# Mean squares of tokens summed straight onto all partitions in an attention and two-layer MLP kernel

## The chip, the core and the metric

The kernel runs on one core of one Trainium2 chip. The metric is the device time of one execution in microseconds (us); the median of three timed runs of the kernel before is 725.94 us (723.27 to 726.9). TensorE is written PE in the profile (PEld are its weight loads), VectorE is DVE, ScalarE is ACT, GpSimd is POOL, and SP issues the DMAs.

## The reference, cut to what matters

Landmark attention over 4 batches, 8 heads and 576 tokens gives one row of 512 numbers for each of 2304 tokens. Each row is divided by its root mean square, then goes through a gated layer, and last through a layer of eight experts for some of the tokens:

```python
x = attn_out.transpose(0, 2, 1, 3).reshape(B * S, H * D)      # 2304 x 512
rms = np.sqrt(np.mean(x * x, axis=-1, keepdims=True) + 1e-06)
xn = x / rms * rms_g
g = xn @ w_gate
silu = g * (1.0 / (1.0 + np.exp(-g)))
x = (silu * (xn @ w_val)) @ w_out                              # then the experts
```

The change is inside the first two lines, for one batch of 576 tokens at a time.

## The kernel before

**Stages.** Attention is never written out as 512 numbers per token. For each batch, `attention(b)` (line 556) leaves a matrix `AT` of 128 partitions by 2 by 576 tokens (heads and landmarks on the partitions) and a small matrix `WT`. The product of `WT` with the weights of the gated layer (`products`, tiles `P`) makes that layer's weights for this batch, so that its matmuls take `AT`, scaled per token, as their moving operand. The scale per token is `rbs`, 128 partitions by 576 tokens: the inverse root mean square of each token, the same on all partitions. `prep(half)` (line 709) multiplies `AT` by `rbs` into `ap` and splits `ap` into a high and a low part (`ap_t`) for one half batch.

The 2304 tokens pass as eight units of 288 (half a batch each). `run_unit` (line 1196) runs the two gated matmuls per chunk of 128 features (`pg`, `pv`, into `h`, split into `h_t`), twelve chunks, then the output projection (`o`, from `h_t` and `wo`, into `x2T`). The attention of the next batch, the products `P` and the routing run as side work between the matmuls of a unit. After the eighth unit a loop over pairs of expert and batch (`ph`, `py`) fills the last 160 us or so.

**The place of the change.** For each batch the last part of `attention` gets squares `sq` whose sum over partitions is 512 times the mean square of a token: two tiles of 128 by 576 in the first batch (`fast`), one in the others. Lines 673 to 680 sum them with the squares as the stationary operand and one column of `onesd` (each 1/512) as the moving one: five groups of tokens, each giving one column of `ps` with tokens on partitions. Lines 681 to 688 take `max` with 0 (not in the first batch), root and reciprocal on 128 by 4 and 64 by 1 numbers. Lines 691 to 703 bring the inverses back onto all partitions: a matmul per group of 128 tokens with the column of `rms` broadcast over 128 columns as the stationary operand and the identity as the moving one, then two copies, of 256 tokens by DVE and 320 by ACT, into `rbs`.

**What sets the order.** The code records instructions with their dependences, and a list scheduler of the framework orders each engine's queue by its own estimates of their lengths. Each engine then runs its queue strictly in that order. The helper `Paced` (line 36) calls every operation from line 58, so nearly all rows of the profile carry L58, and names of tiles tell the places apart. `Paced` also counts estimated lengths, by which `slot` (line 1178) decides how much side work is recorded between the matmuls of a unit. A matmul of two fp32 operands shows as two MATMUL records.

**What the steps touch besides.** `convert_w` and `convert_wout` (lines 768 and 778) turn the 64-bit weights into fp32 with VectorE and ScalarE: TENSOR_SCALAR, SCALAR_TENSOR_TENSOR and TENSOR_TENSOR on `wo`, `wf` and `x` are theirs on VectorE. They fill the stretch up to about 156 us, that is, unit 0. `rsplit` (line 80) casts a tile on ScalarE and subtracts on VectorE or GpSimd. A product `P` takes two PSUM banks of the pool `pb`, which has two, so the next product waits until VectorE has subtracted (`P<-P,P`) both.

Of the kernel before, what the change touches and what calls it, by code (L numbers as in the profile page):

```python
# [6 lines left out]
F32 = mybir.dt.float32  # L7
F32R = mybir.dt.float32r
I32 = mybir.dt.int32
ALU = mybir.AluOpType  # L10
AF = mybir.ActivationFunctionType
# [10 lines left out]
NH = S // 2  # L22
# [40 lines left out]
def attention_moe_kernel(  # L63
# [4 lines left out]
    V, A, G, PE = (  # L68
        Paced(e, busy, n)
        for e, n in (  # L70
            (nc.vector, "V"), (nc.scalar, "A"), (nc.gpsimd, "G"), (nc.tensor, "P")
        )
    )
# [3 lines left out]
    def pool(stack, name, bufs=1, **kw):  # L77
        return stack.enter_context(tc.tile_pool(name=name, bufs=bufs, **kw))
# [37 lines left out]
    sm = pool(pha, "sm", side="right")  # L116

    start, start1 = ExitStack(), ExitStack()
# [6 lines left out]
    def atile(name):  # L125
        if fast:
            return st0.tile([128, S], F32, name=name, tag="wa", bufs=6)
        return at.tile([128, S], F32, name=name, tag="wa", bufs=2)

    def atbank(name):  # L130
        nonlocal nbank
        nbank += 1
        if fast and nbank % 4 < 2:
            return accbank(name)
        if fast and nbank % 4 == 2:
            return bank(name)
        return pa.tile([128, 512], F32, name=name, tag="a")

    def accbank(name):
        return acc.tile([128, 512], F32, name=name, tag="acc")  # L140

    def bank(name):
        return pb.tile([128, 512], F32, name=name, tag="b")
# [5 lines left out]
    ident = const.tile([128, 128], F32, name="ident")  # L149
# [8 lines left out]
    onesd = const.tile([128, 32], F32, name="onesd")  # L158
# [10 lines left out]
    eps = const.tile([128, 1], F32, name="eps")  # L169
# [48 lines left out]
    rbs = big.tile([128, S], F32, name="rbs")  # L218
# [337 lines left out]
    def attention(b, convs=()):  # L556
# [31 lines left out]
        if fast:  # L588
# [25 lines left out]
            for g in range(2):  # L614
                for p in range(2):
                    sq = atile("sq")
                    for t in range(2):
                        ps = atbank("oT")
# [3 lines left out]
                            start=True, stop=True,  # L622
                        )
                        A.activation(sq[:, NH * t : NH * t + NH], ps[:, 0:NH], AF.Square)
                    i = 2 * g + p
                    if i < 2:
                        sqs.append(sq)
                    else:
                        o = sqs[i % 2]
                        V.tensor_tensor(o, o, sq, ALU.add)  # L630
                    yield
        else:
# [29 lines left out]
            for g in range(2):  # L662
                sq = atile("sq")
                for t in range(2):
                    ts = slice(NH * t, NH * t + NH)
                    ps = atbank("sq")
# [3 lines left out]
                yield  # L670
            V.tensor_tensor(sqs[0], sqs[0], sqs.pop(), ALU.add)

        ps = atbank("ms")
        tiles = [(t, 128 if t < 4 else 64) for t in range(5)]
        for t, m in tiles:
            for i, sq in enumerate(sqs):
                PE.matmul(
                    ps[0:m, t : t + 1], sq[:, 128 * t : 128 * t + m], onesd[:, 0:1],
                    start=(i == 0), stop=(i == len(sqs) - 1),
                )  # L680
        rms = sm.tile([128, 5], F32, name="rms")
        for sl in ((slice(0, 128), slice(0, 4)), (slice(0, 64), slice(4, 5))):
            ms = ps[sl]
            if not fast:
                ms = rms[sl]
                V.tensor_scalar(ms, ps[sl], 0.0, None, ALU.max)
            A.activation(rms[sl], ms, AF.Sqrt, bias=eps[sl[0]])
            V.reciprocal(rms[sl], rms[sl])
        yield

        for i, ts in enumerate((tiles[0:2], tiles[2:5])):
            ps = atbank("rb")
            n = sum(m for t, m in ts)
            for t, m in ts:
                o = 128 * (t - 2 * i)
                PE.matmul(
                    ps[:, o : o + m], rms[0:m, t : t + 1].to_broadcast([m, 128]),
                    ident[0:m, 0:m], start=True, stop=True,
                )
            if i:  # L700
                A.copy(rbs[:, 256 : 256 + n], ps[:, 0:n])
            else:
                V.tensor_copy(rbs[:, 0:n], ps[:, 0:n])
        yield


# [513 lines left out]
    def first_convs():  # L1220
        for i in range(NC0):
            convert_w(i)
            yield

    drain(attention(0, first_convs()))
    G.memset(wcat, 0.0)
    SP.dma_start(wcat[:, :, 0:E], w_gate2.rearrange("(c p) e -> p c e", p=128))
# [22 lines left out]
    fast = False  # L1250
    prep(1)
    att = attention(1)
    raw = None

# [41 lines left out]
    for u in range(1, 2 * B):  # L1296
# [24 lines left out]
        if half == 0 and b + 1 < B:  # L1321
            att = attention(b + 1)
# [69 lines left out]
```

## Time and profile before

| | us |
|---|---|
| median of the timed runs | 725.94 |
| lowest and highest | 723.27, 726.9 |
| the profiled execution | 730.47 |
| its span | 728.7 |
| PE busy | 667.1 (92%) |
| DVE busy | 459.2 (63%) |
| ACT busy | 295.1 (41%) |

The profiled execution is 0.6% above the median; 1.8 us of its time lie outside the span. Busy shares are over the whole span, and the stages differ: up to about 85 us PE has little to do, up to 156 us (unit 0) the conversions of weights fill DVE, and later PE is busy nearly all the time.

### The profile page before, as it was taken

Reading aid. Unit: us, or ns where it says so; the run is one execution under the profiler, and the core shown is the slowest. Engines: PE = TensorE matmul, PEld = TensorE weight load, DVE = VectorE, ACT = ScalarE, POOL = GpSimd, SP = SyncE. Lnnn points to the kernel's source line nnn. Section 1 sums busy time; section 2 is a strip of 40 time slices with the busy share of each in tenths; the row PEclk is TensorE's granted clock in tenths of the full one; section 3 lists DMA queues with packets and bytes.
Section 4 is the critical chain, followed back from the end, with each engine's and each line's share of the span. In section 5 each row is a group of like instructions: output and inputs, shape, how many; then the busy total and the mean of one; then the engine's idle time right before and its main releaser. Section 6 shows DMA issues by size and latency. Waiting matters only on the chain. (4 is left out here: it accounts for less than half of the span.)

```text
span 728.7 us, 13382 instructions
## 1 busy us (share of the span) xinstructions
PE 667.1 (92%) x4961; PEld 573.5 (79%) x4961; DVE 459.2 (63%) x1016; ACT 295.1 (41%) x641; POOL 145.1 (20%) x162
## 2 busy tenths in 40 slices
PE   5468799789999899999999999999999999997997
PEld 5257367678877599977898897899889988986985
DVE  5984888978887577886467966261553463352451
ACT  0773887753314431433341344240443243241340
POOL 4000024313200140220040130040362023021120
PEclk8765799899999999999999999999999999998999
DMA  8686464573125842226732107230541375462344
GB/s 284 216 248 227 143 217 152 176 180 100 46 86 117 196 128 75 93 67 149 187 84 66 64 20 157 69 75 1 166 139 62 101 218 173 130 201 95 128 140 156
DMA packets 79435, 97.12 MB, mean 133 GB/s; under 512 B 16016, under 2 KB 58000, under 8 KB 79376
## 3 DMA queue, kind: packets, MB, share of 16 engines
q1 hardware_dynamic: 79376, 96.33, 44.9%
q8 instruction: 37, 0.61, 0.4%
q14 instruction: 22, 0.18, 0.1%
HBM read 76.97 MB, written 19.34 MB: 132 GB/s over the span
## 5 line engine op out<-in xcount | busy, mean ns | idle before, releaser
L58 PE MATMUL o<-h_t,wo 128*128 128x288 f32 x1152 | 169.6, 303 | 9.2 <-ACT wo L58 3.8
L58 PEld LDWEIGHTS o<-h_t,wo 128*128 128x128 f32 x1152 | 157.9, 191 | 19.2 <-issue 6.7
L58 POOL TENSOR_TENSOR h_t<-h,h_t 128x288 fp32r<-128x288 f32 x96 | 82.2, 860 | 399.9 <-ACT h_t L58 363.8
L58 PE MATMUL pg<-ap_t,P 128*128 128x288 f32 x576 | 104.1, 306 | 3.6 <-DVE h L58 1.8
L58 PE MATMUL pv<-ap_t,P 128*128 128x288 f32 x576 | 98.8, 301 | 2.7 <-DVE h L58 2.4
L58 PEld LDWEIGHTS pg<-ap_t,P 128*128 128x128 f32 x576 | 83.2, 189 | 17.6 <-issue 10.3
L58 PEld LDWEIGHTS pv<-ap_t,P 128*128 128x128 f32 x576 | 82.8, 189 | 8.8 <-DVE h L58 4.1
L58 PE MATMUL ph<-xsh,P 128*128 128x288 f32 x384 | 80.5, 303 | 4.5 <-PEq L1354 4.5
L58 PEld LDWEIGHTS ph<-xsh,P 128*128 128x128 f32 x384 | 64.0, 194 | 5.4 <-issue 5.4
L58 DVE SCALAR_TENSOR_TENSOR h<-h,pg 128x288 f32<-128x288 f32 x96 | 42.5, 447 | 26.3 <-ACT h L58 25.2
L58 PE MATMUL ph<-xsl,P 128*128 128x288 f32 x192 | 57.9, 302 | 0.0
L58 ACT ACTIVATE h<-pg 128x288 f32<-128x288 f32 x96 | 38.9, 410 | 42.4 <-PE pg L58 39.1
L58 ACT CAST h_t<-h 128x288 fp32r<-128x288 f32 x96 | 40.8, 430 | 32.6 <-DVE h L58 32.0
L58 PE MATMUL py<-wo,h_t 128*128 128x512 f32 x210 | 51.6, 395 | 0.3 <-DVE h_t L58 0.3
L58 PEld LDWEIGHTS py<-wo,h_t 128*128 128x128 f32 x210 | 39.3, 188 | 10.2 <-issue 0.8
L58 DVE TENSOR_TENSOR h<-h,pv 128x288 f32<-128x288 f32 x96 | 42.4, 446 | 5.9 <-PE pv L58 3.0
L58 DVE STREAM_TRANSPOSE T<-kq 64x576 f32<-64x576 f32 (+1 forms) x40 | 35.6, 889 | 9.0 <-DMA kq<-in_q_dram 4.6
L58 DVE TENSOR_TENSOR P<-P,P 128x512 fp32r<-128x512 f32 x48 | 31.7, 685 | 12.5 <-ACT P L58 12.1
L58 ACT CAST P<-P 128x512 fp32r<-128x512 f32 x48 | 26.3, 588 | 31.8 <-PE P L58 31.6
L58 PEld LDWEIGHTS ph<-xsl,P 128*128 128x128 f32 x192 | 37.4, 195 | 0.1
L58 POOL TENSOR_TENSOR P<-w1r,P 128x512 fp32r<-128x512 f32 x16 | 21.4, 1341 | 66.3 <-ACT P L58 66.3
L58 DVE SCALAR_TENSOR_TENSOR old<-py,mc,old 128x512 f32<-128x512 f32 (+1 forms) x18 | 13.5, 749 | 31.4 <-PE py L58 31.2
(230 smaller groups left out, 967.2 us busy)
## 6 DMA issues: line engine op xcount, KB each, us to landing
wl<-wg_d SPq DMA_DIRECT2D x36, 256.0 KB, 4.7
wr<-wv_d SPq DMA_DIRECT2D x32, 256.0 KB, 4.8
w1r<-in_moe_w_dram SPq DMA_DIRECT2D x32, 256.0 KB, 3.2
wr<-in_moe_w_gate_dram SPq DMA_DIRECT2D x6, 1024.0 KB, 6.6
wr<-in_moe_w_val_dram SPq DMA_DIRECT2D x6, 1024.0 KB, 6.1
wo<-in_moe_w_dram SPq DMA_DIRECT2D x24, 256.0 KB, 5.3
kq<-in_k_dram SPq DMA_DIRECT2D x8, 576.0 KB, 4.3
kq<-in_q_dram SPq DMA_DIRECT2D x8, 576.0 KB, 4.0
```

What stands on the lines that cost most here:

```text
L58: return f(*args, **kw)
```

## The change

The sum is done with the operands the other way round: the column of `onesd`, broadcast over 128 columns, is the stationary operand and the squares are the moving one. Each output partition then holds the mean square of every token, so the result is at once on all partitions, in two halves of 288 tokens. Root and reciprocal are taken on 128 by 288 numbers, into `rbs`. The matmuls with the identity, the two copies and the tile `rms` are gone.

```diff
-        ps = atbank("ms")
-        tiles = [(t, 128 if t < 4 else 64) for t in range(5)]
-        for t, m in tiles:
+        for t in range(2):
+            ts = slice(NH * t, NH * t + NH)
+            ps = atbank("ms")[:, 0:NH]
             for i, sq in enumerate(sqs):
                 PE.matmul(
-                    ps[0:m, t : t + 1], sq[:, 128 * t : 128 * t + m], onesd[:, 0:1],
+                    ps, onesd[:, 0:1].to_broadcast([128, 128]), sq[:, ts],
                     start=(i == 0), stop=(i == len(sqs) - 1),
                 )
-        rms = sm.tile([128, 5], F32, name="rms")
-        for sl in ((slice(0, 128), slice(0, 4)), (slice(0, 64), slice(4, 5))):
-            ms = ps[sl]
+            ms = ps
             if not fast:
-                ms = rms[sl]
-                V.tensor_scalar(ms, ps[sl], 0.0, None, ALU.max)
-            A.activation(rms[sl], ms, AF.Sqrt, bias=eps[sl[0]])
-            V.reciprocal(rms[sl], rms[sl])
-        yield
-
-        for i, ts in enumerate((tiles[0:2], tiles[2:5])):
-            ps = atbank("rb")
-            n = sum(m for t, m in ts)
-            for t, m in ts:
-                o = 128 * (t - 2 * i)
-                PE.matmul(
-                    ps[:, o : o + m], rms[0:m, t : t + 1].to_broadcast([m, 128]),
-                    ident[0:m, 0:m], start=True, stop=True,
-                )
-            if i:
-                A.copy(rbs[:, 256 : 256 + n], ps[:, 0:n])
-            else:
-                V.tensor_copy(rbs[:, 0:n], ps[:, 0:n])
+                ms = rbs[:, ts]
+                V.tensor_scalar(ms, ps, 0.0, None, ALU.max)
+            A.activation(rbs[:, ts], ms, AF.Sqrt, bias=eps)
+            V.reciprocal(rbs[:, ts], rbs[:, ts])
         yield
```

The scheduler makes a new order of everything near these places. Three of them follow.

On VectorE, first batch, before unit 0 (`wo<-wr` and `wo<-wo,s` are conversions of weights). Before:

```order
L58 TENSOR_SCALAR wo<-wr 128x1024
L58 RECIPROCAL rms<-rms 128x4
L58 RECIPROCAL rms<-rms 64x1
L58 SCALAR_TENSOR_TENSOR wo<-wr,wo 128x1024
L58 COPY rbs<-rb 128x256
L58 TENSOR_TENSOR ap<-AT,rbs 128x288 x4
L58 TENSOR_TENSOR ap_t<-ap,ap_t 128x288 x4
L58 TENSOR_TENSOR wo<-wo,s_873 128x1024
L58 TENSOR_TENSOR P_690<-P,P_690 128x512 x2
```

Now:

```order
L58 TENSOR_SCALAR wo<-wr 128x1024
L58 SCALAR_TENSOR_TENSOR wo<-wr,wo 128x1024
L58 RECIPROCAL rbs<-rbs 128x288 x2
L58 TENSOR_TENSOR wo<-wo,s_858 128x1024
L58 TENSOR_TENSOR ap<-AT,rbs 128x288 x3
L58 TENSOR_TENSOR ap_t<-ap,ap_t 128x288 x3
L58 TENSOR_TENSOR ap<-AT,rbs 128x288
L58 TENSOR_TENSOR P_675<-P,P_675 128x512 x2
```

The reciprocals stand behind one conversion, a second conversion stands between them and `ap`, and the copy is gone.

On VectorE at the end of unit 0, where `x2T<-o` is the first work on the output of the unit, `ln` and `lmk` are the landmarks of the next batch's second group of heads, and `mx`, `nmx` and `csum` its softmax. Before:

```order
L58 TENSOR_REDUCE ln<-kq 128x64
L58 TENSOR_TENSOR wo<-x_1234,wo 128x512
L58 STREAM_TRANSPOSE lmk_1511<-ln 128x64
L58 TENSOR_SCALAR x2T<-o 128x288 x2
L58 TENSOR_REDUCE mx<-sq 128x1 x2
L58 TENSOR_SCALAR nmx<-mx 128x1
L58 TENSOR_SCALAR csum<-cs 128x1
```

Now:

```order
L58 TENSOR_TENSOR wo<-x_1219,wo 128x512
L58 STREAM_TRANSPOSE lmq_1398<-ln 128x64
L58 TENSOR_TENSOR bdq<-lmq_1398,maskj 128x256
L58 TENSOR_SCALAR x2T<-o 128x288 x2
L58 TENSOR_REDUCE mx<-sq 128x1 x2
L58 TENSOR_SCALAR nmx<-mx 128x1
L58 TENSOR_REDUCE ln<-kq 128x64
L58 TENSOR_SCALAR csum<-cs 128x1
L58 STREAM_TRANSPOSE lmk_1496<-ln 128x64
```

A reduction over the keys has moved from before the last conversion of unit 0 to behind `nmx`, into unit 1.

On VectorE in the last batch, where `P<-P,P` are the subtractions that free the banks of the products. Before:

```order
L58 TENSOR_SCALAR rms<-ms 128x4
L58 TENSOR_SCALAR rms<-ms 64x1
L58 TENSOR_TENSOR P_690<-P,P_690 128x512 x2
L58 RECIPROCAL rms<-rms 128x4
L58 RECIPROCAL rms<-rms 64x1
L58 COPY rbs<-rb 128x256
L58 SCALAR_TENSOR_TENSOR h<-h,pg 128x288
L58 TENSOR_TENSOR ap<-AT,rbs 128x288 x2
L58 TENSOR_TENSOR P_690<-P,P_690 128x512
```

Now:

```order
L58 TENSOR_SCALAR rbs<-ms 128x288 x2
L58 TENSOR_TENSOR P_675<-P,P_675 128x512
L58 SCALAR_TENSOR_TENSOR h<-h,pg 128x288
L58 TENSOR_TENSOR h<-h,pv 128x288
L58 RECIPROCAL rbs<-rbs 128x288 x2
L58 TENSOR_TENSOR P_675<-P,P_675 128x512
L58 TENSOR_TENSOR ap<-AT,rbs 128x288 x2
L58 TENSOR_TENSOR P_675<-P,P_675 128x512
```

Both reciprocals stand directly ahead of the subtraction that frees the first bank of a product, and `ap` stands ahead of the one that frees the second.

On TensorE the `ms` rows become four matmuls of 128x288 in the first batch and two in each of the others, and the five `rb` matmuls are gone everywhere. Behind the fourth batch's place, around 460 us, the orders of all engines are the same as before but for two neighbours on VectorE that change places.

## Rows read from the trace of the kernel before

**Rows 1.** The page: busy time per engine, then three strips of 40 slices.

```profile
PE 667.1 (92%) x4961; PEld 573.5 (79%) x4961; DVE 459.2 (63%) x1016; ACT 295.1 (41%) x641; POOL 145.1 (20%) x162
PE   5468799789999899999999999999999999997997
DVE  5984888978887577886467966261553463352451
PEclk8765799899999999999999999999999999998999
```

**Rows 2.** Busy time by stretches: PE, PEld, DVE, ACT, POOL, PEclk, DMA share.

```profile
100.00:110.00 10.00, 10.00 (x45) 4.95 (x42) 8.37 (x13) 8.56 (x17) 2.43 (x3) 1.00 0.58 212
140.00:150.00 10.00, 7.68 (x47) 7.21 (x45) 10.00 (x16) 8.58 (x16) 2.82 (x2) 0.85 0.57 188
440.00:460.00 20.00, 20.00 (x206) 16.08 (x207) 11.72 (x25) 10.46 (x20) 1.76 (x1) 1.00 0.73 159
```

**Rows 3.** Timeline, first batch (start, us, instruction, idle before); conversions by form.

```profile
75.42 2.05 PE L58 MATMUL ms<-onesd,sq 128*128 128x1 f32 x18 [1.36 <-DVE sq L58]
78.25 0.21 DVE L58 RECIPROCAL rms<-rms 128x4 f32<-128x4 f32 x2
78.48 2.69 PE L58 MATMUL rb<-ident,rms 128*128 128x128 f32 x10 [1.01 <-DVE rms L58]
81.21 0.42 ACT L58 COPY rbs<-rb 128x320 f32<-128x320 f32 x1 [0.73 <-PE rb L58]
81.67 2.63 DVE L58 TENSOR_TENSOR ap<-AT,rbs 128x288 f32<-128x288 f32 x4 [1.50 <-ACT rbs L58]
92.91 0.45 DVE L58 SCALAR_TENSOR_TENSOR h<-h,pg 128x288 f32<-128x288 f32 x1
L58 DVE TENSOR_TENSOR wo<-wo,s 128x1024 f32<-128x1024 f32 x12 | 14.6, 1218 | 1.9 <-ACT wo L58 1.9
```

**Rows 4.** Reciprocals of two lengths by tile: count, min/median/max in ns.

```profile
L58 DVE RECIPROCAL arec<-asum x8: 250/258/268, 36.2 to 415.6; 128x18 f32<-128x18 f32 x8
L58 DVE RECIPROCAL rs<-rs x4: 177/181/191, 260.6 to 569.1; 128x6 f32<-128x6 f32 x4
```

**Rows 5.** Timeline and groups by form: instructions of the added shapes.

```profile
216.52 1.24 PE L58 MATMUL sq<-AT,gram 128*128 128x288 f32 x4
L58 DVE TENSOR_SCALAR x2T<-o 128x288 f32<-128x288 f32 x16 | 7.1, 451 | 36.7 <-PE o L58 36.6
L58 ACT ACTIVATE sq<-oT 128x288 f32<-128x288 f32 x8 | 3.2, 410 | 5.2 <-PE oT L58 5.2
```

**Rows 6.** Timeline, batches two to four: sums and broadcasts on TensorE.

```profile
221.05 1.26 PE L58 MATMUL ms<-onesd,sq 128*128 128x1 f32 x10 [1.00 <-DVE sq L58]
225.07 1.52 PE L58 MATMUL rb<-ident,rms 128*128 128x128 f32 x10
...
332.59 2.23 PE L58 MATMUL rb<-ident,rms 128*128 128x128 f32 x10
...
440.40 1.16 PE L58 MATMUL ms<-onesd,sq 128*128 128x1 f32 x10
444.34 1.52 PE L58 MATMUL rb<-ident,rms 128*128 128x128 f32 x10
```

**Rows 7.** Third batch: P products in the timeline, and a window with the clock.

```profile
330.75 1.91 PE L58 MATMUL P<-wr,WT 64*32 64x256 f32 x18
332.00:333.00 1.00, 1.00 (x4) 0.41 (x3) 0.00 (x0) 0.00 (x0) 0.00 (x0) 0.50 0.00 0
```

**Rows 8.** Timeline: a P subtraction, batch four; a P weight load, batch two.

```profile
447.70 0.70 DVE L58 TENSOR_TENSOR P<-P,P 128x512 fp32r<-128x512 f32 x1
242.33 0.62 PEld L58 LDWEIGHTS P<-wr,WT 64*32 64x32 f32 x32 [0.54 <-DMA wr<-wv_d]
```

**Rows 9.** Timeline of VectorE around the end of unit 0.

```profile
152.65 2.21 DVE L58 TENSOR_REDUCE ln<-kq 128x64 f32<-128x1152 f32 x1
161.11 0.21 DVE L58 TENSOR_SCALAR csum<-cs 128x1 f32<-128x1 f32 x1 [1.14 <-ACT C L58]
```

## The prediction

> **What bounds the kernel now.** I read the page first [rows 1]. PE is busy for 92% of the span and DVE for 63%, but the strips show three stages. In the first four slices, up to some 73 us, PE is at 4 to 8 tenths. In the next ones DVE stands at 7 to 9 tenths. From the middle on PE stands at 9 and DVE falls to 2 to 6. So a microsecond of PE saved late is worth a microsecond, and one of DVE added early may cost one. The change does both. The windows sharpen this [rows 2]. Between 100 and 110 us PE is full (10.00 of 10) and DVE has 8.37. Between 140 and 150 us DVE is full (10.00) and PE has 7.68: the output projection of unit 0 waits there for converted weights. At 440 to 460 us, around the last place that changes, PE is full (20.00 of 20) and DVE has 11.72.
>
> The timeline of the first batch [rows 3] shows the chain that the change rebuilds: the sums end at 77.47 us, the reciprocals stand at 78.25, the broadcast matmuls run from 78.48 to 81.17, the ACT copy ends at 81.63, and `ap` starts at 81.67 after DVE idled 1.50 us. The first `h` of unit 0 on DVE is at 92.91.
>
> **What is removed and added, per batch.** Removed on PE are ten MATMUL records of sums and ten of broadcasts (the first batch has twenty of sums), on DVE two short reciprocals and a copy of 0.42 us (short ones 0.21 together [rows 3]; the copy is put at the length of ACT's), on ACT two short roots and a copy of 0.42. Added on PE are four records of 128x288 (eight in the first batch): four of that shape took 1.24 us at full clock [rows 5]. Added on ACT are two roots at 0.41, the price of a square of that shape; ACT ends about even. Added on DVE, in the last three batches, are two `max` at 0.45 from PSUM [rows 5], and in all four two reciprocals of 288 numbers.
>
> **The reciprocal decides.** The trace has none that long. The two lengths that it has give a price per number [rows 4]: 258 ns for 18 and 181 for 6, so 77 ns for 12 numbers, 6.4 ns each, and 258 + 270 x 6.4 = 1.99 us for 288. I take 1.95, rounding down for the shorter samples. The ends of the samples give (250 - 191)/12 = 4.9 to (268 - 177)/12 = 7.6 ns, that is, 1.6 to 2.3 us. A floor is the 0.45 us of another DVE instruction of this shape [rows 5], which would hold if the slope came from start-up and not from the numbers; I give it little, since a start-up would lie in the 6 as well as in the 18. So two cost 3.9 us of DVE per batch. The Trainium skill speaks against the change more strongly: "VectorE: DVE Perf Modes", section "First, the fixed hardware budget", says the reciprocal is an iterative division with a repeat count of 8, and its specifications give a clock of 0.96 GHz. As an estimate from that page, 8 cycles per number are 8.3 ns and 2.4 us plus the fixed part, 2.55 us each; the measured slope of 6.4 is lower. By that page the sum below would be about -1.0 in place of -4.7.
>
> **The start (first batch to unit 1).** In the new order DVE runs one conversion, the two reciprocals, another conversion (1.22 [rows 3]), then `ap`. It gains 3.9 us of work, loses 0.21 + 0.42, and the 1.50 us in which it waited for the ACT copy are filled. The extra conversion ahead of `ap` is work done earlier and comes back. So DVE reaches the same point 3.9 - 0.63 - 1.50 = 1.8 us later, and the first `h` at 92.9 + 1.8 + 1.2, about 96. PE's own sums matter little there, since the root waits for ACT. PE is full in the window from 100 us [rows 2], so the lag stays. What gives it back is a move of the scheduler's: a reduction of 2.21 us [rows 9] no longer stands ahead of the last conversion of unit 0, in the stretch where DVE is full. 1.8 - 2.2 = -0.4 at the end of unit 0. The reduction now stands behind `nmx`, where DVE idled 1.14 us [rows 9]; `csum` comes 2.2 - 1.1 = 1.1 later, which only the next `h` and later the weighting of values wait for, while PE has matmuls of unit 1 to run: I take 0. Bounds: -2.2 (DVE's waits for ACT and PE in unit 0 swallow the lag) to 3.3 + 1.1 = +4.4 (all of it is paid and the reduction's leaving saves nothing). I take **-0.4**.
>
> **Second batch.** PE loses 1.26 + 1.52 and gains 1.24 [rows 5, 6]: -1.54. Of this I give back 0.7, since the chain to `ap` now holds 3.9 + 0.9 us of DVE in place of short instructions, 1.5 of matmuls and the copies, and unit 2's first gated matmuls stand close behind. The later products wait for weights from DRAM anyhow (0.54 us idle at 242.33 [rows 8]), so it could all be lost. **-0.8**, bounds -1.5 and 0.
>
> **Third batch.** The sums are put at the 1.26 of the second. The broadcasts took 2.23 us there, against 1.52 in the neighbours [rows 6], and the 18 P records before them 1.91 us; the granted clock in the window is 0.50, the 1.2 GHz level [rows 7]. The level fell after a stretch with sums of one column and small P products; the new sums have 288 columns and the broadcasts are gone, so I expect 2.4 GHz to stay. That gives 1.26 + 2.23 - 1.24 = 2.25 on sums and broadcasts, and half of the 1.91, about 0.9, on P. Against this: DVE's next subtraction of P, which frees a bank for the next product, stands behind the reciprocals; I give back 0.5. **-2.65**, bounds -3.15 and -1.0 (the low level stays and falls on other matmuls).
>
> **Fourth batch.** PE loses 1.16 + 1.52 and gains 1.24: -1.44 [rows 5, 6]. Behind the sums, which end near 441.5, DVE has two `max` (0.9), a P (0.7), two on `h` (0.9), two reciprocals (3.9) and the P (0.7) that frees the first bank: 448.6, against 448.40 before [rows 8]. The second bank needs two `ap` at 0.66 [rows 3] and a P more: 450.6. PE arrives about 1.4 earlier than before and waits in front of these two products; I give back 0.6. **-0.85**, bounds -1.44 and 0.
>
> **The sum.** -0.4 - 0.8 - 2.65 - 0.85 = -4.7 us. From the profiled execution, 730.47, this gives 725.8; the median is 4.5 us below that execution, and from the median, 725.94, I predict **721.2 us**. Behind the fourth place nothing is reordered and PE bounds, so what is gained by 460 us should reach the end.
>
> **The rivals.** (1) *VectorE as the bound, slower.* If DVE is full from 77 to 231 us, it hands on all that is added: 3.9 - 0.63 = 3.3 in the first batch and 3.9 + 0.9 - 0.2 - 0.2 - 0.4, about 4.0, in the second, 7.3 in all; less 2.65 and 0.85 for the last two, that is +3.8, 729.7, and 731 with reciprocals at 2.3. It decides from the point at which DVE's idle time in unit 0 (1.6 us of 10 at 100 to 110 [rows 2]) is no longer spare because its chain with ACT runs late throughout. For it: the full window at 140. Against it: PE, not DVE, is full at 100. (2) *The gain is swallowed.* The clock falls anyway and the second batch waits for its weights: -0.4 + 0 - 1.0 - 0.4 = -1.8, 724.1. For it speaks the DMA wait [rows 8]. (3) *Dear reciprocals*, 2.3 us, the upper end of the samples: 0.7 more of DVE per place, of which the start pays 0.7 and the others some 0.55 each: -4.7 + 2.35 = -2.35, 723.6. The page named above goes this way and further. (4) *Cheap reciprocals*, 0.45 us: no give-backs, the start at its bound: -2.2 - 1.54 - 3.15 - 1.44 = -8.3, 717.6; then the change does all that its matmul count says. Against it stands the slope [rows 4].
>
> **How the numbers follow.** Forecast 0.48, rival (1) 0.13, (2) 0.17, (3) 0.12, (4) 0.10. About 0.5%, 3.6 us, is what a measurement of this kernel can tell from no change. The forecast's centre lies 1.1 beyond it, so I count 0.35 of its 0.48 as faster and 0.13 as same. Faster: 0.35 + 0.10 = 0.45. Same: 0.13 + 0.17 + 0.12 = 0.42. Slower: 0.13. The bounds of the places add up to -8.3 and +3.4; they rarely all fall one way, so the range goes from 717.5, which keeps rival (4), to 728.5, which leaves out rival (1) and little else.
>
> **What would show it.** Reciprocals of 128x288 near 1.95 us, eight of them; `ap` of the first batch near 84.6 and the first `h` near 96; the last conversion of unit 0 within 2 us of where it was; a granted clock of 1.00 near 330; four `ms` records in about 1.24 us and idle time of PE in front of P in the third and fourth batch. A reciprocal below 1 us or above 2.4 would overthrow the sum, and so would a first `o` of unit 1 more than 3 us late.

## The result, and the profile of the changed kernel

The changed kernel takes 718.11 us (median of four runs, 715.35 to 719.8) against 726.42 for the kernel before beside it (723.27 to 729.91). The two medians lie 8.3 us apart. The ratio of the runs is 0.9866, with a 95% interval of 0.9829 to 0.9903: about 9.7 us faster, 7 to 12.4. Two later comparisons gave 0.9840 [0.9809, 0.9871] and 0.9854 [0.9811, 0.9897]. The direction of the forecast was right and the time lies in its range, but the gain is about twice the 4.7 us that the sum gave.

The page of the changed kernel, its line of busy times and the strips that answer to [rows 1]:

```profile
PE 651.2 (91%) x4891; PEld 562.2 (79%) x4891; DVE 471.5 (66%) x1012; ACT 294.9 (41%) x637; POOL 145.6 (20%) x162
PE   5388599798999799999999999999999999997997
DVE  6985999988987775888458968360634464352451
PEclk9766799999999999999999999999999999998999
```

PE has 15.9 us less to do and DVE 12.3 more. The groups by form (count, busy us, mean ns) give the prices of the new instructions:

```profile
L58 DVE RECIPROCAL rbs<-rbs 128x288 f32<-128x288 f32 x8 | 15.0, 1921 | 0.0
L58 DVE TENSOR_SCALAR rbs<-ms 128x288 f32<-128x288 f32 x6 | 2.4, 446 | 0.0
L58 ACT ACTIVATE rbs<-rbs,eps 128x288 f32<-128x288 f32 x6 | 2.9, 529 | 1.9 <-DVE rbs L58 1.9
```

A reciprocal of 288 numbers takes 1.92 us, where the forecast had worked out 1.95 from [rows 4]. The root takes 0.53 instead of 0.41. The first batch on VectorE, as the timeline shows it, answers to [rows 3]:

```profile
74.75 3.76 DVE L58 RECIPROCAL rbs<-rbs 128x288 f32<-128x288 f32 x2
78.42 1.16 DVE L58 TENSOR_TENSOR wo<-wo,s 128x1024 f32<-128x1024 f32 x1
79.50 1.90 DVE L58 TENSOR_TENSOR ap<-AT,rbs 128x288 f32<-128x288 f32 x3
...
90.37 0.86 DVE L58 SCALAR_TENSOR_TENSOR h<-h,pg 128x288 f32<-128x288 f32 x2
...
145.26 0.67 DVE L58 TENSOR_TENSOR wo<-x,wo 128x512 fp32r<-128x512 f32 x1
...
146.47 0.81 DVE L58 TENSOR_SCALAR x2T<-o 128x288 f32<-128x288 f32 x2
```

To compare stages between kernels I cut each timeline of VectorE at the same instructions: the second addition of squares in the first batch (S1), the first `h`, the first `x2T` (end of unit 0), the additions of squares of the other batches (S2, S3, S4), and the last `x2T` of the seventh unit. Each entry is the difference of two start times. The kernels below "changed" come from the experiments; a number behind a name counts the profile.

| kernel | start to S1 | S1 to `h` | `h` to `x2T` | to S2 | S2 to S3 | S3 to S4 | to unit 7's end | rest |
|---|---|---|---|---|---|---|---|---|
| before | 74.62 | 18.29 | 63.05 | 64.29 | 106.50 | 112.74 | 67.63 | 221.58 |
| changed | 69.83 | 20.54 | 56.10 | 63.78 | 107.66 | 108.78 | 66.50 | 220.41 |
| changed, 2 | 70.11 | 20.54 | 56.03 | 64.06 | 107.31 | 108.82 | 66.53 | 220.50 |
| changed, 3 | 69.98 | 20.54 | 56.04 | 63.87 | 108.17 | 108.78 | 66.73 | 220.39 |
| first_only | 71.83 | 20.55 | 56.11 | 63.81 | 109.44 | 111.48 | 67.91 | 221.67 |
| later_only | 71.11 | 18.18 | 63.14 | 63.84 | 108.71 | 108.82 | 66.52 | 221.58 |
| new_in_old_order | 71.57 | 20.26 | 62.35 | 64.33 | 106.57 | 111.51 | 67.66 | 221.75 |
| old_in_new_order_b | 71.17 | 19.27 | 56.06 | 63.89 | 107.03 | 111.18 | 67.62 | 219.58 |
| all_old_order | 70.11 | 20.31 | 61.93 | 64.33 | 112.19 | 113.28 | 68.31 | 220.44 |

Nothing is changed before S1, and the other profiles with old code there show 70 to 72.5 us. The 4.8 us between the first two rows of that column are the spread of single executions, and most of why the profiled execution of before, 730.47, lies above its median. From S1 on the two differ by 654.1 - 643.8 = 10.3 us, near what the comparisons say (8.3 by the medians, 9.7 by the ratio). It splits into +2.25 and -6.95 (unit 0, -4.7 together, forecast -0.4), -0.5 up to S2, +1.2 (second batch, forecast -0.8), -4.0 (third, -2.65), -1.1 (fourth, -0.85) and -1.2 in the rest. The rest is 219.6 to 222.0 in kernels with old code, so I read nothing from it.

So the place where the forecast missed most is unit 0. The wait view of VectorE between the first `h` and the first `x2T` (us in total, times, longest) tells half of it. The kernel before:

```profile
DVE h L58 <- ACT h L58: 1.9, 4, 1.1
DVE P L58 <- ACT P L58: 1.6, 3, 0.9
DVE h L58 <- PE pv L58: 1.5, 1, 1.5
```

The changed kernel:

```profile
DVE x L58 <- POOL wo L58: 1.2, 1, 1.2
DVE P L58 <- ACT P L58: 0.7, 1, 0.7
DVE h L58 <- ACT h L58: 0.3, 1, 0.3
```

In the windows of the same stretch (length, then busy times of PE, PEld, DVE, ACT and POOL, and last the clock, the DMA share and GB/s), before and after:

```profile
92.91:155.96 63.05, 53.80 (x301) 41.23 (x301) 57.21 (x91) 47.41 (x85) 20.40 (x18) 0.95 0.55 178
```

```profile
90.37:146.47 56.10, 49.04 (x296) 38.98 (x296) 53.61 (x88) 45.49 (x83) 21.93 (x18) 0.97 0.55 177
```

DVE has 57.21 - 53.61 = 3.6 us less to do there: the reduction of [rows 9] has left (2.2), and a conversion is done earlier (1.2). That was forecast. Its idle time shrank as well, from 5.84 to 2.49, and that was not. PE has 53.80 - 49.04 = 4.8 us less to do there too. Nearly half of that lies in the products, whose 32 records of the same mean length overlap more than before (L58 rows of the same two windows, before and after):

```profile
L58 PE MATMUL P<-wo,WT 128*64 128x512 f32 x32 | 11.2, 613 | 0.0
L58 PE MATMUL P<-wo,WT 128*64 128x512 f32 x32 | 9.0, 611 | 0.1
```

Whether the instructions or their order did all this, the page can't say.

### The profile page after: what moved, and what is told of

Same layout as the page of the kernel before. It is cut to its first block, busy times and chain, and to the rows that moved or that the text cites. A ratio compares the mean times of both kernels' runs of the same rounds, so it can differ in the third digit from the quotient of the medians.

```text
span 713.6 us, 13229 instructions
## 1 busy us (share of the span) xinstructions
PE 651.2 (91%) x4891; PEld 562.2 (79%) x4891; DVE 471.5 (66%) x1012; ACT 294.9 (41%) x637; POOL 145.6 (20%) x162
## 5 line engine op out<-in xcount | busy, mean ns | idle before, releaser
L58 PE MATMUL o<-h_t,wo 128*128 128x288 f32 x1152 | 167.3, 301 | 6.7 <-ACT wo L58 3.1
L58 PEld LDWEIGHTS o<-h_t,wo 128*128 128x128 f32 x1152 | 156.7, 190 | 15.9 <-issue 6.3
L58 POOL TENSOR_TENSOR h_t<-h,h_t 128x288 fp32r<-128x288 f32 x96 | 82.4, 861 | 388.5 <-ACT h_t L58 364.1
L58 PE MATMUL pg<-ap_t,P 128*128 128x288 f32 x576 | 104.1, 307 | 11.2 <-ACT P L58 7.9
L58 PEld LDWEIGHTS pg<-ap_t,P 128*128 128x128 f32 x576 | 83.6, 191 | 24.4 <-issue 14.9
L58 PE MATMUL pv<-ap_t,P 128*128 128x288 f32 x576 | 99.1, 302 | 1.8 <-DVE h L58 0.8
L58 PEld LDWEIGHTS pv<-ap_t,P 128*128 128x128 f32 x576 | 83.2, 190 | 6.5 <-issue 2.2
L58 PE MATMUL ph<-xsh,P 128*128 128x288 f32 x384 | 80.2, 302 | 4.5 <-PEq L1337 4.5
L58 PEld LDWEIGHTS ph<-xsh,P 128*128 128x128 f32 x384 | 63.8, 194 | 5.4 <-issue 5.4
L58 DVE SCALAR_TENSOR_TENSOR h<-h,pg 128x288 f32<-128x288 f32 x96 | 42.7, 448 | 33.1 <-ACT h L58 32.3
L58 ACT ACTIVATE h<-pg 128x288 f32<-128x288 f32 x96 | 39.2, 411 | 49.3 <-PE pg L58 46.6
L58 PE MATMUL ph<-xsl,P 128*128 128x288 f32 x192 | 57.8, 301 | 0.0
L58 ACT CAST h_t<-h 128x288 fp32r<-128x288 f32 x96 | 41.0, 430 | 29.6 <-DVE h L58 28.8
L58 PE MATMUL py<-wo,h_t 128*128 128x512 f32 x210 | 51.4, 395 | 0.0
L58 PEld LDWEIGHTS py<-wo,h_t 128*128 128x128 f32 x210 | 39.5, 188 | 9.5
L58 DVE TENSOR_TENSOR h<-h,pv 128x288 f32<-128x288 f32 x96 | 42.7, 448 | 4.7 <-PE pv L58 1.3
L58 DVE STREAM_TRANSPOSE T<-kq 64x576 f32<-64x576 f32 (+1 forms) x40 | 35.5, 887 | 5.6 <-DMA kq<-in_k_dram 3.8
L58 ACT CAST P<-P 128x512 fp32r<-128x512 f32 x48 | 26.4, 585 | 27.2 <-PE P L58 26.5
L58 PEld LDWEIGHTS ph<-xsl,P 128*128 128x128 f32 x192 | 37.2, 194 | 0.1
L58 DVE TENSOR_TENSOR P<-P,P 128x512 fp32r<-128x512 f32 x48 | 31.9, 688 | 5.7 <-ACT P L58 5.4
L58 POOL TENSOR_TENSOR P<-w1r,P 128x512 fp32r<-128x512 f32 x16 | 21.1, 1318 | 66.6 <-ACT P L58 66.6
L58 DVE SCALAR_TENSOR_TENSOR old<-py,mc,old 128x512 f32<-128x512 f32 (+1 forms) x18 | 13.5, 749 | 31.3 <-PE py L58 31.0
```

The lines of the kernel that those rows point to most:

```text
L58: return f(*args, **kw)
```

## The experiments

The theory after the result (A) was: the gain that was not foreseen lies in unit 0, where DVE's waits close. The rival (B): it lies in TensorE's time and clock in the later batches. All ratios are against the kernel before, run beside each kernel on the same chip, with the 95% interval.

### One part alone

In first_only the first batch takes the new code and the others the old; later_only is the reverse (`if not fast`).

```diff
+        if fast:
+            for t in range(2):
...
+        else:
+            ps = atbank("ms")
...
```

> The new sums, roots and reciprocals in the first batch alone; the other three batches keep the code of the kernel before. Its order is that of the changed kernel up to the sums of the second batch. The prediction's terms give -0.4 us against the kernel before (726). Theory A, that unit 0 gives the unforeseen gain because VectorE's idle time there shrinks and its conversions come earlier: -4 to -5.5, about 721.5, and the first x2T 6 to 7 us sooner after the first h than in the kernel before. Theory B, that the gain comes from TensorE time and clock in the later batches: 0 to -1.

> The new code in the second, third and fourth batch alone; the first batch keeps the code of the kernel before, and the order up to the sums of the second batch is the kernel before's. The prediction's terms give -0.8 - 2.65 - 0.85 = -4.3 us. Theory A: -4 to -5, about 721.5, and the granted clock near 330 us stays at 1.00. Theory B: -8 to -9, about 717.5.

Measured: 724.8 us, 0.9963 [0.9935, 0.9991], and 723.7, 0.9950 [0.9922, 0.9978]. Theory A had put both near 721.5. The sum of the two gains, some 6 us, is less than the whole, so as totals they settle nothing. The table does: S1 to `x2T` is 76.66 in first_only and 81.32 in later_only, against 81.34 before and 76.64 in the changed kernel. The -4.7 comes with the first batch's edit alone. first_only gives some of it back between S2 and S3 (109.44 and, repeated, 108.98 against 106.50), where its code is the old one. The order differs there, and so does the granted clock, 0.98 in both profiles against 1.00; the old code in the old order took 107.75 at 0.98 (ln_late, below).

### More and fewer reciprocals

```diff
-            V.reciprocal(rbs[:, ts], rbs[:, ts])
+            V.tensor_scalar(rbs[:, ts], rbs[:, ts], 0.5, None, ALU.mult)
```

This is cheap_recip, which leaves the inverse out; dear_recip has the line of the reciprocal three times.

> The changed kernel with each reciprocal replaced by a multiplication by 0.5 of the same 128x288 tile, so the inverse is left out; 0.45 us in place of 1.92, 2.9 us of VectorE less per batch. The scheduler orders the work anew. If VectorE's time at these places is paid in full, some 2.9 us at the start and 0.5 to 1 at each other place are gained against the changed kernel, 713 to 715. Theory A, that unit 0 hides it: within 2 us of the changed kernel, 716 to 719.

> The changed kernel with each reciprocal taken three times in a row, so 7.7 us more of VectorE per batch and the same values. The scheduler orders the work anew. If VectorE hands on what it is given (rival 1): +7.7 at the start and some 7 in the second batch, less in the others, 733 or more, slower than the kernel before. Theory A, with 2 to 3 us of VectorE idle time left in unit 0 to swallow it: +4 to +6 at the start and +1 to +3 in each later batch, 725 to 732. If the start's gain has nothing to do with VectorE's time: +3 or less, 721.

cheap_recip took 656.64 us, 0.9025, and tells nothing by that: behind unit 7 it took 162.3 us where all others take some 220, where the loop over experts had less to do (256 + 128 `ph` records on PE against 384 + 192 in the changed kernel): with the inverse left out the routing sees other numbers. Its stages can be read: S1 to `x2T` 78.6 us, longer than the 76.6 of the changed kernel with 2.9 us less of DVE's work. The scheduler had made another order.

dear_recip took 738.56, 1.0145 [1.0105, 1.0185], outside the 725 to 732 of theory A. Against the changed kernel S1 to `h` grew by 8.6 and S2 to S3 by 12; the third and the fourth batch grew by 0.8 and 0. In this order, which the scheduler made anew, VectorE's added time is paid in the first two batches and hidden in the last two.

### Order against instructions

The kernels of this part, and later all_old_order, mix, ln_late, ln_early and rsqrt_act_pinned, have a table of every instruction's place on PE, DVE, ACT and POOL and tie each to the one ahead of it, so that the scheduler has no choice; the DMA queue is left free (in new_in_old_order one load moves by one place, in all_old_order several loads of weights change places in the second and third batch too). Pinning by itself shows no cost: where code and order are those of the kernel before, the pinned kernels take its time (64.33 us against 64.29 from `x2T` to S2).

```diff
+ORDER = {
+    "V": [
...
+    for n, ids in ORDER.items():
+        ins = [LOG[i] for i in ids]
+        for a, b in zip(ins, ins[1:]):
+            tc.add_manual_dep(
+                b, a.name,
...
+                reason="pinned order",
+            )
```

> The new sums, roots and reciprocals in the first batch alone, as in first_only, but every instruction of TensorE, VectorE, ScalarE and GpSimd pinned to its place in the order of the kernel before; the reciprocals stand where the short ones stood. If the unforeseen gain of unit 0 comes from the order that the scheduler made (theory A1): the stretch from the last sq sum to the first x2T is no longer 76.7 us but 81 or more, and the time is 726 to 729, 0 to +2 against the kernel before. If it comes from the instructions themselves, from TensorE's chain being gone (theory A2): 76 to 78.5 us in that stretch and about 724.

> The sums, short reciprocals and broadcasts of the kernel before in all four batches, but every instruction pinned to its place in the order of first_only. A1: the stretch from the last sq sum to the first x2T is 76 us or less, since the order is kept and VectorE has 3.3 us less to do, and the time is 721 to 724. A2: 80 to 82 us in that stretch and 725 to 728.

new_in_old_order: 730.24, 1.0031 [1.0004, 1.0058]. `h` to `x2T` is 62.35 us, not 56.1. With the order goes nearly all of the gain, and what remains is the lag: S1 to `x2T` 82.6, 1.3 more than before.

old_in_new_order: 727.08, 0.9979 [0.9953, 1.0004], with 56.03 us from `h` to `x2T`, but 23.97 from S1 to `h`. That was my own doing. ACT's copy stood right behind the roots and blocked ACT until the broadcasts were done (timeline of ACT):

```profile
80.38 0.43 ACT L404 COPY rbs<-rb 128x320 f32<-128x320 f32 x1 [4.28 <-PE rb L404]
```

and DVE waited 6.30 us behind it for a conversion. With the copy three instructions later:

> The sums, short reciprocals and broadcasts of the kernel before in all batches, every shared instruction at its place in the order of first_only; other than in old_in_new_order ScalarE's copy of the broadcast stands three instructions later and VectorE's copy and short reciprocals where the kernel before has them, so that neither engine blocks itself. A1 (order): last sq sum to first h about 18.5 to 19.5 us, first h to first x2T 56.0, together 74.5 to 75.5, less than the 76.7 of the changed kernel; the time 721 to 725. A2 (instructions): first h to first x2T 60 or more.

718.1, 0.9889 [0.9836, 0.9943]. Its stretch of unit 0, window and waits:

```profile
90.44:146.50 56.06, 48.77 (x295) 38.74 (x296) 53.59 (x87) 45.43 (x83) 21.97 (x18) 0.97 0.54 177
```

```profile
DVE x L404 <- POOL wo L404: 1.2, 1, 1.2
DVE P L404 <- ACT P L404: 0.7, 1, 0.7
DVE h L404 <- ACT h L404: 0.3, 1, 0.3
```

These are the changed kernel's numbers with none of its instructions. (The time came out below the 721 to 725 that A1 gave; the stages were as A1 had them.) `h` to `x2T` is 55.97 to 56.6 us in every kernel that keeps the new order unchanged, with old or new code, and 61.9 to 63.1 in every one with the old order. A1 stands: the order makes 6.2 to 7 us there. The new instructions cost: S1 to `h` is 20.54 with them and 19.27 without in the new order, 20.26 and 18.29 in the old. Over S1 to `x2T` the two terms simply add (DVE's busy time from the window of that stretch):

| S1 to `x2T` | us | DVE busy | DVE idle |
|---|---|---|---|
| old code, old order (before) | 81.34 | 72.68 | 8.66 |
| new code, old order (new_in_old_order) | 82.61 | 75.62 | 6.99 |
| old code, new order (old_in_new_order_b) | 75.33 | 69.98 | 5.35 |
| new code, new order (changed) | 76.64 | 72.96 | 3.68 |

The new instructions cost 1.3 us in either order: 3.0 more of work, of which 1.7 fill idle time. The new order gains 6.0 us with either code: 2.7 less of work ahead of `x2T`, and 3.3 less idle time. The queues of all four engines were exchanged together, so this doesn't say which queue closes the waits.

first_only and this kernel share all code and order from S2 on, and stood at 724.8 and 718.1 on two chips, so both were run again on one.

> first_only once more, beside old_in_new_order_b_2. The two share every instruction and its place from the sums of the second batch on, and in unit 0 the second is 1.3 us shorter; yet they were 724.8 and 718.1 on two chips. If the chips or their runs made the rest of the difference: 1 to 2 us between them here, both near 720 to 724. If something in the programs does: 5 us or more between them again.

> old_in_new_order_b once more, on the chip of first_only_2: 1 to 2 us less than that if the stages of the profile tell the whole, 5 us or more if not.

723.98, 0.9973 [0.9947, 0.9999], and 720.64, 0.9925 [0.9892, 0.9957]: 3.3 us apart, of which unit 0 explains 1.3. The single runs of the second spread from 716.5 to 726.7. Its two profiles are 4.9 us apart from S1 on; in the first the clock is 1.00 in the second and the third batch, in the other 0.98 in both, 1.25 and 1.6 us longer. So such falls of the clock are part of the spread. The other 2 us between the two kernels lie in stretches of equal code and stay open.

### The whole change in either order

> The changed kernel once more, for a second profile and for the spread of its stages. If first_only and later_only add up, -2.7 - 3.6 = -6.3 us against the kernel before; if the earlier comparison holds, -9.7. In the profile: last sq sum to first x2T 76.7 us in either case.

> The new code in all four batches, with every instruction of the four computing engines pinned to its place in the order of the kernel before. By the prediction's terms the three later places keep what comes of fewer matmuls, -1.54, -2.25 and -1.44 at most, less what TensorE waits for the reciprocals that now stand early in VectorE's order, and the start pays up to +3.3: 723 to 728. Theory A1: 5 us or more slower than the changed kernel, 722 to 726. A2, that the order hardly matters: within 2 us of the changed kernel.

> The code of the kernel before in the first batch, the new code in the other three, every shared instruction pinned to its place in the order of the changed kernel. If order and instructions are separate terms, the first stretch takes 74.5 to 75.5 us in place of 76.6 and the rest is the changed kernel's: 1 to 2 us faster than that, about 715, 1.6 to 1.9% faster than the kernel before. If the reciprocals cost nothing in the new order: the time of the changed kernel.

after_again: 715.82, 0.9840 [0.9809, 0.9871]; its stages repeat the first profile's within 0.6 us. all_old_order: 733.37, 1.0077 [1.0050, 1.0103], above what either reading gave it. With every instruction in the old order the change makes the kernel 5.6 us *slower*, and between the two orders of the same instructions lie some 17 us. mix, which keeps the old code in the first batch in the changed kernel's order, took 716.51, 0.9856 [0.9804, 0.9908], 1.3 us less than the changed kernel from S1 to `h` and the same behind: no difference in its median.

all_old_order also shows what the reciprocals do to PE when nothing is moved to cover them. The waits of PE in the second and third batch, timeline:

```profile
230.20 1.06 PE L400 MATMUL P<-wr,WT 64*32 64x256 f32 x2 [2.93 <-DVE P L400]
...
338.78 0.62 PE L400 MATMUL P<-wl,WT 64*32 64x256 f32 x2 [2.86 <-DVE P L400]
```

This is the wait for the subtraction behind the reciprocals that the forecast saw coming and priced at 0.5 to 0.7. Behind the first of the two PE runs some 10 us at the 1.2 GHz level (clock 0.50 from 230.5 to 240.0 us), and from S2 to S3 its clock is 0.95. In the changed kernel's third batch it isn't there: between two products the scheduler put 39 matmuls of the output projection, longer than both reciprocals.

```profile
318.71 1.24 PE L58 MATMUL ms<-sq,onesd 128*128 128x288 f32 x4
319.88 1.12 PE L58 MATMUL P<-wr,WT 64*32 64x256 f32 x32
320.93 5.46 PE L58 MATMUL o<-h_t,wo 128*128 128x288 f32 x39
```

### The one move that the forecast had priced

ln_late is the kernel before, pinned, with the reduction of [rows 9] and its transpose moved to where the changed kernel has them; ln_early is the changed kernel, pinned, with both moved back.

> The kernel before in its own order, with one move: the third reduction of unit 0 (2.2 us) and its transpose (0.2) stand behind the last conversion and the maxima, where the changed kernel has them. By the prediction the first h to first x2T shrinks by 2.2 to 2.4 us, from 63.1 to 60.8, and the last sq sum to first x2T from 81.3 to 79.0. If this move is the whole of the new order's gain: 56 to 57. Time 723.5 to 726 by the former.

> The changed kernel in its own order, with one move the other way: that reduction and its transpose back ahead of the last conversion of unit 0. First h to first x2T from 56.1 to 58.3 by the prediction's price, so that 3.4 of the new order's 7.0 us rest on other moves; 62 to 63 if the move is the whole gain. Time 718 to 721 by the former.

ln_late: 726.84, 1.0011 [0.9982, 1.0039]. `h` to `x2T` shrank by 0.8, not 2.3. The last conversion does start 2.2 us earlier (78.0 against 80.2 us behind S1), but now DVE waits for PE:

```profile
149.86 0.68 DVE L404 TENSOR_TENSOR wo<-x,wo 128x512 fp32r<-128x512 f32 x1
152.26 0.82 DVE L404 TENSOR_SCALAR x2T<-o 128x288 f32<-128x288 f32 x2 [1.72 <-PE o L404]
```

In the old order PE's output projection ends late by itself. Its group in the stretch from `h` to `x2T` (idle before it, and who ended that) shows 9.2 us of waits for conversions and others in the kernel before:

```profile
L58 PE MATMUL o<-h_t,wo 128*128 128x288 f32 x139 | 24.0, 329 | 9.2 <-ACT wo L58 3.8 <-DVE wo L58 2.1 <-POOL wo L58 2.1
```

and 6.7 in the changed kernel:

```profile
L58 PE MATMUL o<-h_t,wo 128*128 128x288 f32 x143 | 23.3, 317 | 6.7 <-ACT wo L58 3.1 <-POOL wo L58 2.8 <-DVE wo L58 0.7
```

ln_early: 725.29, 0.9978 [0.9955, 1.0002]. Here the same move costs 6.7 us in that stretch and 2.6 behind it, because in the new order DVE gets to the reduction before its keys have come:

```profile
143.18 2.23 DVE L400 TENSOR_REDUCE ln<-kq 128x64 f32<-128x1152 f32 x1
149.73 2.08 DVE L400 TENSOR_REDUCE ln<-kq 128x64 f32<-128x1152 f32 x1 [4.32 <-DMA kq<-in_k_dram]
```

So the move is worth 0.8 us in one order and 9 in the other. Neither of my two readings was met: it isn't 2.2 us of a sum, nor the whole gain by itself.

### The reciprocals' price with the order held

One activation (inverse root of the magnitude) takes the place of root and reciprocal; rsqrt_act_pinned keeps the changed kernel's order.

```diff
-            A.activation(rbs[:, ts], ms, AF.Sqrt, bias=eps)
-            V.reciprocal(rbs[:, ts], rbs[:, ts])
+            A.activation(rbs[:, ts], ms, AF.Abs_reciprocal_sqrt, bias=eps)
```

> The changed kernel with root and inverse in one ScalarE activation (inverse root of the magnitude), no reciprocal on VectorE; the scheduler orders anew. If VectorE's 3.8 us per batch are hidden by the changed kernel's order: within 3 us of it, up or down by what the new order does. If they are paid: 4 us faster or more at the start alone, 712 or less.

> As rsqrt_act, with every other instruction pinned to its place in the order of the changed kernel, so that the eight reciprocals are all that is missing. The price of the reciprocals with the order held: by the prediction 3.9 at the start and about 0.5 at each later place, 5.4 us less than the changed kernel, 711. If the new order hides them in the later batches altogether: 2 to 3 us less, from the start alone, 714. If they are hidden throughout: 0.

> Root and inverse in one ScalarE activation, every other instruction in the changed kernel's order, once more beside it: by the stages of its first profile 3.1 us less than the changed kernel behind the first sq sums (640.6 against 643.8), so 711 to 715; 0 if the two were apart only by their chips.

> The changed kernel a third time, on the chip of rsqrt_act_pinned_2: 714 to 718.

Measured: 713.52, 0.9826 [0.9775, 0.9877]; 713.4, 0.9822 [0.9772, 0.9872]; 714.87, 0.9811 [0.9768, 0.9854]; and the changed kernel beside the last, 717.28, 0.9854 [0.9811, 0.9897]. The medians' intervals overlap. The stages don't: from S1 on both profiles of the pinned kernel take 640.6 and 641.1 us against 643.8 to 644.5. Some 3.2 us go with the reciprocals in the changed kernel: 1.2 from S1 to `h` (19.37), 2 between S2 and S3 (105.61 and 105.43), 0.3 in the third batch, 0.1 in the fourth. Of the 2, some 1.3 are a stretch at the low clock, told below, that the changed kernel has there and the pinned one hasn't; that the reciprocals bring it on is not shown. The two kernels with one activation are the fastest that were run.

## Why the prediction was right and wrong

**The reading of the page** holds but for one strip: from the middle on DVE's digits run from 1 to 9, not from 2 to 6, and the windows of [rows 2] carry the argument.

**The reciprocal** was right: 1.92 us for a forecast 1.95. The slope from 18 to 288 numbers is (1921 - 258)/270 = 6.2 ns. The estimate from the Trainium skill ("VectorE: DVE Perf Modes", section "First, the fixed hardware budget": a repeat count of 8) was 2.55 us, and the measurement decides against it.

**The start is the term that failed**, -0.4 forecast and -4.7 measured. Its first half was nearly right: the first `h` was put 3.0 us later (1.8 and a conversion of 1.2) and came 2.25 later; in the old order, new_in_old_order, 2.0. The second half was wrong, and the prediction's own sign shows it: the last conversion was to stay within 2 us of where it was, and it starts 4.7 us earlier behind S1 (75.4 against 80.2). The forecast took the order between `h` and `x2T` to be the old one but for one reduction and one conversion, 2.2 + 1.2 = 3.4 us, and the stretch shrank by 7.0. The missing 3.4 is DVE's idle time: its waits for `h` and `P`, 5.0 us before, are 1.0 in the new order. In the sum's own terms, the lag of 1.8 measured 1.3 in either order, and the term of -2.2 for what the new order gives back measured -6.0 with either code: 2.7 of work and 3.3 of idle time that the forecast put at nothing. The new order was known before the result, and DVE's queue differs from the old one in 16 places between `h` and `x2T`, while I read two of them. The bound of -2.2 was therefore no bound: it allowed the waits to swallow the lag, but not that they close by reordering. And the price of 2.2 for the reduction doesn't exist by itself, as ln_late (0.8) and ln_early (some 9) show.

**The second batch** has the wrong sign, -0.8 forecast, +0.8 to +1.7 measured in three profiles against the one of the kernel before. PE does 0.9 us less (102.32 to 101.46) but waits more. Waits of PE from S2 to S3 in the changed kernel:

```profile
PE lp L58 <- DVE P L58: 1.7, 1, 1.7
PE lg L58 <- DVE P L58: 1.4, 1, 1.4
PE P L58 <- DMA wr<-wv_d: 1.2, 2, 0.9
```

The forecast named both, DVE's chain and the weights from DRAM, as rival (2) did; before, this view had 1.3 for `lg`, 1.2 for `P` and none for a DMA. But the waits don't turn the sign: the first two and the one for the DMA stand in rsqrt_act_pinned as well (1.7, 1.4 and 1.1), and that kernel gains 0.9 and, repeated, 1.1 against before. The changed kernel reaches the matmuls `x2t`, some 36 us behind S2 on PE, 0.5 to 1.0 us earlier than the kernel before (36.06, 35.48 and 35.62 us in three profiles against 36.52), which is what was forecast. Behind it PE is full, and the clock falls. The windows from there to PE's next matmuls `sq`, in the kernel before, the changed one and rsqrt_act_pinned, with a window and a row from inside the fall:

```profile
256.77:287.52 30.75, 30.75 (x251) 30.00 (x249) 23.26 (x56) 7.38 (x20) 7.56 (x9) 1.00 0.42 112
246.31:278.67 32.36, 32.36 (x252) 31.71 (x250) 21.19 (x53) 6.88 (x20) 7.77 (x9) 0.95 0.45 117
244.32:275.34 31.02, 31.02 (x251) 30.18 (x249) 21.11 (x53) 7.21 (x20) 7.65 (x9) 1.00 0.46 121
247.50:250.00 2.50, 2.50 (x12) 2.50 (x12) 2.27 (x10) 0.86 (x3) 0.54 (x1) 0.50 0.91 294
248.17 1.64 PE L58 MATMUL pv<-ap_t,P 128*128 128x288 f32 x6
```

Six such records take 0.96 us at 1.00. So 1.3 of the 1.6 us that are lost here go with a fall to the 1.2 GHz level, at this place in all three profiles of the changed kernel and in neither of the two of the pinned one; the forecast had no term for it. The reciprocals themselves cost 0.7 up to the matmuls `cT`, early in the batch (20.7 us behind S2 against 20.0). Why the level falls here is open: mix, with the changed kernel's code and order in this batch, has its fall 9 us earlier. The old code isn't free of it either. In its old order, S2 to S3 took 106.50 and 106.57 at 1.00 (before, new_in_old_order) and 107.75 at 0.98 (ln_late), and against the last of these the changed kernel, 107.3 to 108.2, shows no clear loss.

**The third batch** came out at -4.0 against -2.65, for partly other reasons. The low clock of [rows 7] was taken as a property of the old code. It is one of some executions: of eight profiles with old code at this place four have it (S3 to S4 112.7 to 112.9) and four don't (111.2 to 111.5). The P records of the place and a window of new_in_old_order, where the clock is 1.00:

```profile
327.94 0.62 PE L404 MATMUL P<-wr,WT 64*32 64x256 f32 x2
329.08 1.05 PE L404 MATMUL P<-wr,WT 64*32 64x256 f32 x18
330.06 1.52 PE L404 MATMUL rb<-ident,rms 128*128 128x128 f32 x10
331.51 0.65 PE L404 MATMUL P<-wr,WT 64*32 64x256 f32 x12
```

```profile
329.00:332.00 3.00, 3.00 (x42) 1.82 (x40) 0.66 (x4) 0.39 (x1) 0.00 (x0) 1.00 0.20 53
```

So the drop costs about 1.4 us where it comes, near the 1.6 that I took, but it comes only half of the time; the profile of the kernel before was one that had it. The changed kernel shows 1.00 and 108.8 in all three profiles. Without the drop the place gains 2.4 to 2.7: the sums and broadcasts (1.26 + 1.52 - 1.24 = 1.54), and 1.2 that the forecast didn't have, because nothing cuts the P products any more: 0.62 + 1.05 + 0.65 for 32 records in pieces, 1.12 for 32 in a row. The 0.5 given back for the reciprocals is 0, thanks to the order.

**The fourth batch**, -0.85 forecast, measured -1.1: the size fits. The reason that was given for the 0.6 doesn't: the waits in front of its two products stay under 0.2 us each. What keeps the gain below the 1.44 of the matmuls is not shown, so the fit is in part luck.

**The rivals.** "VectorE as the bound" (+3.8) was given 0.13, and its total is near what the instructions do in the old order, 5.6 us slower. Its terms are not. The start pays 0.9 from S1 to `x2T`, not 3.3; the second batch pays 5.7, not 4.0, by PE's wait for the subtraction and the low clock behind it; and the third and fourth, where the rival kept gains of 2.65 and 0.85, lose 0.5 and 0.7. What kept this from happening is an order that the scheduler chose anew. Shown is that the order carries the gain of unit 0; which of its many moves there carries how much is not settled, since the one tried by itself was worth 0.8 or 9 us depending on the others. Why first_only and old_in_new_order_b_2 are 2 us further apart than unit 0 makes them is open too.

## What to carry to other kernels

Where a list scheduler orders the queues, an edit is two changes, its instructions and the new order, and the second can be the larger: here +5.6 us and some -17. To tell them apart, pin the new instructions into the old order, and the old into the new. Before forecasting, list the waits of the engine that bounds each stage: whatever idle time stands there is what a new order can win or lose, and a moved instruction has no price of its own while the order around it is free to change.

## What the runs showed of the hardware

- The old code of the third batch ran at the 1.2 GHz level for some 3 us in four profiles of eight, and at 2.4 GHz in the others, after a stretch with sums of one column and small products: 1.91 against 1.05 us for the same eighteen records. Two of the programs were profiled twice there, and each had the fall once (S3 to S4 111.48 and 112.90, 111.18 and 112.77 us).
- RECIPROCAL of 128x288 fp32 numbers takes 1.92 us on DVE, 4.3 times a TENSOR_SCALAR of that shape (0.446), while the inverse root in one activation takes 0.53 on ACT, as long as the root alone.
- Small P matmuls (64x256, 32 columns of weights) cost less in a row: 32 records in 1.12 us, and 2.32 where other matmuls cut them into three pieces.
